# Seven 256-column products in place of eight in the output product of layer two, for the second to fourth block of tokens

## The chip, the cores and the metric

The kernel runs on one core of one Trainium2 chip. The time is that of one execution on the device, in microseconds (us); the median of three runs of the kernel before is 1085.78 us (1084.87 to 1085.96). The engines are named as the profile names them: PE is TensorE (matmul), PEld its weight loads, DVE VectorE, ACT ScalarE, POOL GpSimd, and SPq the queue of SyncE, from which nearly all transfers are started.

## The reference

Attention with a compressive memory gives 2304 tokens of 512 features; two gated layers follow. The change lies in the last line, the product of layer two's 1536 gated features with `w_out`.

```python
def _moe_ref(x, w_gate, w_val, w_out):          # layer one; 2304 tokens, 512 -> 1536 -> 512
    gate = 1.0 / (1.0 + np.exp(-(x @ w_gate)))
    val = x @ w_val
    return (gate * val @ w_out).astype(np.float32)

def _moe2_ref(x, w_a, w_b, w_out):              # layer two, same sizes
    a = x @ w_a
    b = x @ w_b
    return (a * b @ w_out).astype(np.float32)

def reference(**kwargs):
    ...
    x = _moe_ref(x=x, **moe_kwargs)
    return _moe2_ref(x=x, **moe2_kwargs)
```

## The kernel before

**Tiling.** The tokens are cut into five blocks: four of 512 (one per batch row) and a fifth of 256, which holds the first 64 tokens of each of the four. The 1536 inner features are twelve chunks of 128. Every fp32 operand is split into a high part (a rounded copy, written by ACT) and a low part (the rest, a subtraction on DVE), both in one "unit" of 128 x 2 x 512 values; each product is then three matmuls, high by high, high by low and low by high. PE's order is written out by hand (`manual_schedule`); on the other engines a scheduler sets the order of what the program records.

**Stages.** The attention fills the first 330 us. From there PE does the two layers. The input products of both layers are already done with seven products for eight (`strassen`, over pairs of token blocks, pairs of chunks and halves of the features); the gated features go out to DRAM tensors `gd` and come back for the output product. Weights come in pieces (`piece`: a transfer into `st`, two ACT operations, two DVE operations, an addition on POOL (L850), then the high part by ACT (L811) and the low part by DVE (L805)). Tasks like these are advanced from `hook`, which the PE program calls between its products; `ev`, `tile_t` and `bank` hand out the 10 buffers of gated features and results, the 11 work tiles and the 8 PSUM banks.

**The output product of layer two** is `outs(1, ...)`. It goes through the five blocks, and in each through the twelve chunks. `g_load` (L1230) brings a chunk of 128 features by 512 tokens back from `gd`, `g_split` cuts it into high part (ACT, L1237) and low part (DVE, L1238), up to three chunks ahead of the PE. `out_rows` (L1254 to L1256) then does, for each of the four groups of 128 tokens (two in the fifth block), three matmuls: the token group is the stationary operand, and all 512 output features of the weight chunk are the moving one.

```python
for f, o in enumerate(mo):
    r = slice(f * P, f * P + P)
    pe.matmul(o, lhsT=t[:, 0, r], rhs=w[:, 0], start=first, stop=False)
    pe.matmul(o, lhsT=t[:, 0, r], rhs=w[:, 1], start=False, stop=False)
    st["gate"] = pe.matmul(o, lhsT=t[:, 1, r], rhs=w[:, 0], start=False, stop=last)
```

The four PSUM banks of a block stay open over all twelve chunks; `c_fin` then copies them out (ACT L1321, DVE L1319) and sends them to the output (L1324). This stage runs from 927.7 us to the end of the span.

Of the kernel before, what the change touches and what calls it, by code (L numbers as in the profile page):

```python
# [9 lines left out]
F32 = mybir.dt.float32  # L10
# [9 lines left out]
def kernel(  # L20
# [721 lines left out]
    with tc.manual_schedule(engines={mybir.EngineType.PE}):  # L742
# [71 lines left out]
        def piece(layer, c, kind, half, mixed):  # L814
# [44 lines left out]
                return  # L859
            yield (half, 0, 0, 2)  # L860
            t = high_part(f"w{kind}", f, half)
            yield (0, 0, 0)
            low_part(t, f)
            ws[layer, c, kind] = t
            freed.append("t")

        uses, due, behind, held = {}, {}, [], []

        def used(key):
            uses[key] -= 1  # L870
# [12 lines left out]
        def mix(layer, g, kind):  # L883
            ka, kb = (layer, g, kind), (layer, g + MATE[layer], kind)
            yield (0, 2, 0)
            a, b, x, y = wf[ka], wf[kb], slice(0, 256), slice(256, 512)
            m, n = tile_t("mx"), tile_t("mx")
            vec.tensor_tensor(out=m[:, x], in0=b[:, x], in1=a[:, x], op=ALU.subtract)
            vec.tensor_tensor(out=n[:, x], in0=b[:, y], in1=b[:, x], op=ALU.subtract)
            yield (0, 0, 0)  # L890
            vec.tensor_tensor(out=n[:, y], in0=b[:, y], in1=m[:, x], op=ALU.subtract)
            vec.tensor_tensor(out=m[:, y], in0=a[:, y], in1=n[:, y], op=ALU.subtract)
            for key, f in (((layer, g, kind, 0), n), ((layer, g, kind, 1), m)):
                wf[key], uses[key], due[key] = f, 1, turn_[0] + 1
            used(ka)
            used(kb)

        def x_load(layer, b, kk):
            t = tile_t("xt")
# [332 lines left out]
        def g_split(layer, blk, c):  # L1232
# [5 lines left out]
            vec.tensor_tensor(  # L1238
                out=t[:, 1, 0:n], in0=f, in1=t[:, 0, 0:n].bitcast(F32), op=ALU.subtract
            )  # L1240

# [15 lines left out]

        def outs_of(layer):

            return [(blk, c) for blk in range(B + 1) for c in (every if layer else upper)]  # L1260

        def outs(layer, rate):

            seq = outs_of(layer)
            ahead = 2
            for m, (blk, c) in enumerate(seq):
                if m + 5 < len(seq):
                    g_load(layer, *seq[m + 5])
                while ahead < min(m + 4, len(seq)):
                    settle_free()  # L1270
                    key = (layer, seq[ahead][1], 2)
# [3 lines left out]
                    g_split(layer, *seq[ahead])  # L1275
                    ahead += 1
                if c == seq[0][1]:
                    mo = [bank() for f in range(KD if not layer else cols(blk) // P)]
                t, n = gs.pop((layer, blk, c)), cols(blk)
                if layer:  # L1280
                    out_rows(mo, c, t, c == 0, c == NCH - 1)
                else:
                    st["gate"] = out_wide(
                        blk, mo, c, t[:, 0, 0:n], t[:, 1, 0:n], c == MA, c == NCH - 1
                    )
                drop(t)
                if blk == B:
                    drop(ws[layer, c, 2])
                if c == NCH - 1:
                    (c_fin if layer else b_fin)(blk, mo)  # L1290
                hook(rate)

        def part_fin(blk, mo):
# [115 lines left out]
            wave(1, g)  # L1409
        for c in every:  # L1410
            task(piece(1, c, 2, "LH"[c % 2], False))

        ends = []
        early(B - 1, 4)
        early(B, 2)
        for layer in H2:
            for g, h in PAIRS[layer]:
# [10 lines left out]
            outs(layer, 6 if layer else 3)  # L1428
        bctx.close()


# [29 lines left out]
```

## Time and profile before

| | us |
|---|---|
| median of 3 runs | 1085.78 (1084.87 to 1085.96) |
| the profiled execution | 1085.2 |
| its span, first to last instruction | 1083.4 |
| PE busy | 1055.7 (97%) |
| DVE busy | 664.9 (61%) |
| ACT busy | 552.2 (51%) |
| POOL busy | 193.6 (18%) |
| layer two's output product, 927.7 us to the end | 155.7 |

The profile's busy time of a matmul includes the time in which its results drain while the next one already runs, so the pace of PE is read from the distance between starts and not from a single duration. The same holds for operations that stand back to back on DVE and ACT. An idle time in brackets behind a row of the timeline names what ended it.

### The profile page before, as it was taken

The numbers are of one execution on the slowest core, as the hardware profiler recorded it, in microseconds if no ns is written. First come the engines' busy times: TensorE is split into PE (matmuls) and PEld (weight loads), VectorE is DVE, ScalarE is ACT, GpSimd is POOL, SyncE is SP. The second block draws the span as 40 slices with busy tenths as digits, with TensorE's granted clock in tenths as the row PEclk, the third lists the DMA queues.
The fourth block names the chain that finished last, engine by engine and source line by source line (L and its number), as shares of the span: only waits on it lengthen the run. The fifth ranks groups of instructions, "written<-read, shape, count | busy, mean of one in ns | idle before, by whom it ended". The sixth has DMA issues, their size and how long they took to land.

```text
span 1083.4 us, 16215 instructions
## 1 busy us (share of the span) xinstructions
PE 1055.7 (97%) x5624; PEld 844.6 (78%) x5624; DVE 664.9 (61%) x1407; ACT 552.2 (51%) x1173; POOL 193.6 (18%) x204
## 2 busy tenths in 40 slices
PE   6989999999999999999999999999999999999997
PEld 4656677777777888888888888888888888888886
DVE  5897764565443988576578554976565578721221
ACT  5887765765744565544555333554344446431221
POOL 2443431232220302110221000221011013200000
PEclk9999999999999999999999999999999999999999
DMA  7665434333114434232368745343243244542233
GB/s 167 154 172 156 121 93 109 82 85 91 45 67 128 139 115 134 94 122 102 127 217 291 256 145 175 127 129 106 74 136 116 69 145 177 190 155 95 81 112 92
DMA packets 147202, 140.61 MB, mean 130 GB/s; under 512 B 73776, under 2 KB 107696, under 8 KB 147120
## 3 DMA queue, kind: packets, MB, share of 16 engines
q1 hardware_dynamic: 145648, 139.25, 41.0%
q8 instruction: 44, 0.72, 0.3%
q10 hardware_dynamic: 1472, 0.33, 0.1%
q14 instruction: 38, 0.31, 0.1%
HBM read 97.00 MB, written 42.54 MB: 129 GB/s over the span
## 4 chain that ended last, share of the span: by engine, by line
PE 82%; DVE 8%; ACT 3%; DMA 3%; issue 1%; POOL 1%; SPq 1%; POOLq 0%; DVEq 0%; ACTq 0%
PE gv L450 16%; PE gv L451 16%; PE gv L449 15%; PE gv L1256 5%; PE gv L1255 5%; PE gv L1254 4%; PE sc L195 4%; PE m L449 3%; PE tp L369 3%; PE m L451 3%; PE m L450 3%; PE tp L330 2%; PE tp L343 2%; DVE s L224 2%; PE tp L363 1%
## 5 line engine op out<-in xcount | busy, mean ns | idle before, releaser
L450 PE MATMUL gv<-xm,w 128*128 128x512 f32 (+1 forms) x752 | 272.7, 363 | 1.0 <-DVE xm L805 1.0
L451 PE MATMUL gv<-xm,w 128*128 128x512 f32 (+1 forms) x752 | 272.7, 363 | 0.0
L449 PE MATMUL gv<-xm,w 128*128 128x512 f32 (+1 forms) x752 | 272.3, 362 | 0.0
L850 POOL TENSOR_TENSOR wt<-wt,st 128x512 int32<-128x512 int32 x60 | 89.3, 1495 | 528.7 <-DVE wt L846 294.5
L450 PEld LDWEIGHTS gv<-xm,w 128*128 128x128 f32 x752 | 141.5, 188 | 24.1 <-DVE xm L805 1.5
L449 PEld LDWEIGHTS gv<-xm,w 128*128 128x128 f32 x752 | 141.5, 188 | 22.8 <-ACT ev L1069 0.4
L451 PEld LDWEIGHTS gv<-xm,w 128*128 128x128 f32 x752 | 141.6, 188 | 22.0
L1069 ACT ACTIVATE ev<-gv 128x512 f32<-128x512 f32 (+1 forms) x168 | 91.2, 561 | 85.2 <-PE gv L451 84.9
L1073 DVE TENSOR_TENSOR ev<-gv,ev 128x512 f32<-128x512 f32 x120 | 80.6, 685 | 70.3 <-PE gv L451 39.0
L1238 DVE TENSOR_TENSOR gs<-ev,gs 128x512 fp32r<-128x512 f32 (+1 forms) x100 | 63.4, 664 | 52.7 <-ACT gs L1237 52.2
L1237 ACT ACTIVATE gs<-ev 128x512 fp32r<-128x512 f32 (+1 forms) x100 | 56.1, 584 | 72.8 <-DMA ev<-gd 46.0
L1256 PE MATMUL gv<-w,gs 128*128 128x512 f32 x216 | 85.5, 396 | 0.1
L1255 PE MATMUL gv<-w,gs 128*128 128x512 f32 x216 | 85.0, 394 | 0.0
L1254 PE MATMUL gv<-w,gs 128*128 128x512 f32 x216 | 84.2, 390 | 0.0
L229 ACT ACTIVATE s<-s,mx 128x320 f32<-128x320 f32 (+3 forms) x128 | 77.6, 607 | 10.3 <-DVE mx L224 10.2
L224 DVE CUSTOM_DVE_ANT_0 s<-sc,mask 64x64 f32<-64x64 f32 (+4 forms) x160 | 68.9, 481 | 16.3 <-PE sc L195 16.3
L149 ACT ACTIVATE aw<-tp 128x512 f32<-128x512 f32 (+2 forms) x112 | 55.6, 513 | 43.7 <-PE tp L330 36.9
L840 ACT ACTIVATE wt<-st 128x512 f32<-128x512 f32 x60 | 39.5, 667 | 58.7 <-DMA st<-in_moe_w_out_dram 19.6
L195 PE MATMUL sc<-kt,qt 64*128 64x320 f32 (+4 forms) x384 | 61.4, 433 | 1.0 <-DVE mx L224 1.0
L451 PE MATMUL gv<-gs,w 128*128 128x512 f32 (+1 forms) x160 | 59.6, 373 | 0.0
L450 PE MATMUL gv<-gs,w 128*128 128x512 f32 (+1 forms) x160 | 59.4, 371 | 0.0
L449 PE MATMUL gv<-gs,w 128*128 128x512 f32 (+1 forms) x160 | 58.9, 368 | 0.0
(134 smaller groups left out, 1824.2 us busy)
## 6 DMA issues: line engine op xcount, KB each, us to landing
gd<-ev SPq DMA_DIRECT2D x80, 256.0 KB
ev<-gd SPq DMA_DIRECT2D x80, 256.0 KB
st<-in_moe_w_out_dram SPq DMA_DIRECT2D x24, 512.0 KB
st<-in_moe_w_gate_dram SPq DMA_DIRECT2D x12, 512.0 KB
st<-in_moe_w_val_dram SPq DMA_DIRECT2D x12, 512.0 KB
st<-in_moe_w_a_dram SPq DMA_DIRECT2D x12, 512.0 KB
st<-in_moe_w_b_dram SPq DMA_DIRECT2D x12, 512.0 KB
x<-rd SPq DMA_DIRECT2D x32, 144.0 KB
```

The source lines that it names most:

```text
L195: st["anchor"] = pe.matmul(scs[e][0:m, SC0[i] + a:SC0[i] + z], lhsT=st["q", p][r, r0:r0 + m], rhs=st["k", p][r, a:z], start=True, stop=True,)
L224: st["pace"] = vec.tensor_tensor_reduce(out=s, in0=scs[e][0:m, SC0[i]:SC0[i] + w], in1=mask[0:m, c:c + w], scale=1.0, scalar=BIG, op0=ALU. ...
L229: st["apace"] = act.activation(out=o, in_=s, func=AF.Exp, scale=-1.0, bias=mx[0:m, i:i + 1], accum_out=sms[p % 2][0:m, i:i + 1, e],)
L449: pe.matmul(o, lhsT=w[:, 0, ws_], rhs=xh, start=first, stop=False, skip_group_check=True)
L450: pe.matmul(o, lhsT=w[:, 0, ws_], rhs=xl, start=False, stop=False, skip_group_check=True)
L451: return pe.matmul(o, lhsT=w[:, 1, ws_], rhs=xh, start=False, stop=last, skip_group_check=True)
L850: pool.tensor_tensor(out=c32, in0=c32, in1=lo, op=ALU.add)
L1069: act.activation(out=t[:, 0:n], in_=src[:, 0:n], func=func)
L1073: st["gate"] = vec.tensor_tensor(out=t, in0=src, in1=t, op=ALU.add)
L1254: pe.matmul(o, lhsT=t[:, 0, r], rhs=w[:, 0], start=first, stop=False)
L1255: pe.matmul(o, lhsT=t[:, 0, r], rhs=w[:, 1], start=False, stop=False)
L1256: st["gate"] = pe.matmul(o, lhsT=t[:, 1, r], rhs=w[:, 0], start=False, stop=last)
```

## The change

Only layer two's output product is changed, and in it only the second, third and fourth block. A pair of chunks g and g + 6 is taken together: the two chunks, the two halves of the block's tokens (256 each) and the two halves of the output features (256 each) make a two by two by two block product, which takes eight half products in the form before and seven in the new one (Winograd's form). Each of the seven has its own PSUM bank, open over the six pairs of a block; in a bank, two groups of 128 tokens by 256 features lie side by side. A half product is two token groups by three matmuls of 256 columns, so a pair is 42 matmuls of 256 columns (`seven`, L1355) where it was 24 of 512. The first and the fifth block keep `out_rows`.

What goes with it:

- `mix_out`: for each of the six pairs, two mixed weight units (`wo`), from four 256-wide DVE operations (L911, L912, L915, L916), two high parts and two low parts. Their input, the weights in fp32, is kept in new DRAM tensors: `piece` stores it to `wd` (L863, behind the POOL addition), and `mix_out` loads it again (L907, L908). The six tasks may start from the second chunk of the first block on.
- `halves` in place of `g_split`: two mixed tiles u and v from four 256-wide DVE operations (L1324 to L1327), then high and low parts (L1331, L1332) of 256 columns for the first chunk and of 512 for the second chunk, u and v. The loads run two pairs ahead, `halves` one pair ahead.
- `seven_fin` in place of `c_fin`: in the last pair of a block each bank is taken out as soon as its product ends: one ACT copy (`keep`), seven DVE additions from PSUM (L1377), eight stores of 128 x 256 to the output (L1383).

```diff
+            if layer:
+                nc.sync.dma_start(out=wd[c], in_=f)
+                due[layer, c, kind] = turn_[0] + 3
...
+        def mix_out(g):
+            h = g + MATE[1]
+            yield (0, 4, 0)
+            a, b, m, n = (tile_t("mo") for _ in range(4))
+            x, y = slice(0, 256), slice(256, 512)
+            nc.sync.dma_start(out=a, in_=wd[g])
+            nc.sync.dma_start(out=b, in_=wd[h])
+            yield (0, 0, 0, 2)
+            with tc.issue_after(st["split"].ins):
+                vec.tensor_tensor(out=m[:, x], in0=a[:, y], in1=a[:, x], op=ALU.subtract)
+                vec.tensor_tensor(out=n[:, y], in0=b[:, y], in1=a[:, y], op=ALU.subtract)
+            yield (0, 0, 0)
+            with tc.issue_after(st["split"].ins):
+                vec.tensor_tensor(out=n[:, x], in0=b[:, y], in1=m[:, x], op=ALU.subtract)
+                vec.tensor_tensor(out=m[:, y], in0=b[:, x], in1=n[:, x], op=ALU.subtract)
+            freed.extend("tt")
+            for k, f in enumerate((n, m)):
...
+                t = high_part("wo", f, "H")
...
+                low_part(t, f)
+                wo[g, k] = t
...
+        def halves(blk, g):
...
+            vec.tensor_tensor(out=v[:, x], in0=a[:, y], in1=b[:, y], op=ALU.add)
+            vec.tensor_tensor(out=u[:, x], in0=v[:, x], in1=a[:, x], op=ALU.subtract)
+            vec.tensor_tensor(out=u[:, y], in0=a[:, x], in1=a[:, y], op=ALU.subtract)
+            vec.tensor_tensor(out=v[:, y], in0=b[:, x], in1=u[:, x], op=ALU.subtract)
+            gs[1, blk, g] = []
+            for f, n in ((a, 256), (b, 512), (u, 512), (v, 512)):
+                t = take("gs", "A")
+                act.activation(out=t[:, 0, 0:n], in_=f[:, 0:n], func=AF.Copy)
+                vec.tensor_tensor(
+                    out=t[:, 1, 0:n], in0=f[:, 0:n], in1=t[:, 0, 0:n].bitcast(F32),
+                    op=ALU.subtract,
+                )
...
+            jobs = (
+                (1, a, 0, wg, 0), (6, u, 0, n, 0), (2, b, 0, wh_, 0), (7, u, 256, n, 256),
+                (5, v, 0, m, 0), (3, v, 256, wh_, 256), (4, b, 256, m, 256),
+            )
+            for k, (i, t, at_, w, wc) in enumerate(jobs):
...
+                for r in H2:
+                    q_ = slice(at_ + r * P, at_ + r * P + P)
+                    for z, (th, wl_) in enumerate(((0, 0), (0, 1), (1, 0))):
+                        st["gate"] = pe.matmul(
+                            mo[i][:, 256 * r:256 * r + 256], lhsT=t[:, th, q_],
+                            rhs=w[:, wl_, wc:wc + 256], start=first and not r and not z,
+                            stop=last and r == 1 and z == 2, skip_group_check=True,
+                        )
+                if last:
+                    seven_fin(blk, i, mo)
...
+                while loaded < len(seq) and loaded <= m + (5 if len(seq[loaded]) == 2 else 2):
...
+                while ahead < loaded and ahead <= m + (3 if len(seq[ahead]) == 2 else 1):
```

**PE, where the first block ends and the second begins.** `gv` are PSUM banks, `w2` the weight chunks, `gs` the split features, `wo` the mixed weights. Before:

```order
L1255 MATMUL gv_9419<-w2_9372,gs_9553 128x512
L1256 MATMUL gv_9419<-w2_9372,gs_9553 128x512
L1254 MATMUL gv_9636<-w2_8884,gs_9570 128x512
L1255 MATMUL gv_9636<-w2_8884,gs_9570 128x512
L1256 MATMUL gv_9636<-w2_8884,gs_9570 128x512
```

and now (L1282 to L1284 are `out_rows`):

```order
L1283 MATMUL gv_9443<-w2_9395,gs_9617 128x512
L1284 MATMUL gv_9443<-w2_9395,gs_9617 128x512
L1355 MATMUL gv_9757<-w2_8896,gs_9687 128x256 x6
L1355 MATMUL gv_9764<-wo_9561,gs_9693 128x256 x6
L1355 MATMUL gv_9771<-w2_9263,gs_9690 128x256 x6
L1355 MATMUL gv_9778<-wo_9561,gs_9693 128x256 x6
L1355 MATMUL gv_9789<-wo_9605,gs_9696 128x256 x6
L1355 MATMUL gv_9796<-w2_9263,gs_9696 128x256 x6
L1355 MATMUL gv_9803<-wo_9605,gs_9690 128x256 x6
L1355 MATMUL gv_9757<-w2_9109,gs_9745 128x256 x6
L1355 MATMUL gv_9764<-wo_9563,gs_9751 128x256 x6
```

The second block's work is now seven rows of six narrow matmuls a pair, into seven banks; the second pair begins with the row before the last.

**DVE, at the same place.** The two COPY rows take the first block's results out of PSUM, so whatever stands behind them comes after that block's last matmuls. Before:

```order
L1238 TENSOR_TENSOR gs_9633<-ev_9585,gs_9633 128x512
L1319 COPY ev_9622<-gv_9417 128x512
L1319 COPY ev_9628<-gv_9419 128x512
L1238 TENSOR_TENSOR gs_9671<-ev_9631,gs_9671 128x512
L1238 TENSOR_TENSOR gs_9688<-ev_9652,gs_9688 128x512
```

and now (`gs_9751` and `gs_9754` are u and v of the second pair):

```order
L916 TENSOR_TENSOR mo_9731<-mo_9730,mo_9732 128x256
L1474 COPY ev_9714<-gv_9441 128x512
L1474 COPY ev_9720<-gv_9443 128x512
L805 TENSOR_TENSOR wo_9723<-mo_9567,wo_9723 128x512
L805 TENSOR_TENSOR wo_9810<-mo_9613,wo_9810 128x512
L1324 TENSOR_TENSOR ev_9740<-ev_9677,ev_9679 128x256
L1326 TENSOR_TENSOR ev_9739<-ev_9677 128x256
L1325 TENSOR_TENSOR ev_9739<-ev_9740,ev_9677 128x256
L1327 TENSOR_TENSOR ev_9740<-ev_9679,ev_9739 128x256
L805 TENSOR_TENSOR wo_9812<-mo_9655,wo_9812 128x512
L1332 TENSOR_TENSOR gs_9751<-ev_9739,gs_9751 128x512
```

Between the copies and the second pair's u stand three low parts of mixed weights and four mixing operations, where there was one low part per chunk before.

**The queue of SP, about the end of the input products.** `wd` is the new store of fp32 weights, `mo` its loads. Now:

```order
L863 DMA wd9_3925<-wt_9291 128x512
L1187 DMA gd1_1_5_3985<-ev_9352 128x512
L1258 DMA ev_9432<-gd1_0_5_3973 128x512
L1187 DMA gd1_3_5_4009<-ev_9381 128x512
L863 DMA wd10_3926<-wt_9314 128x512
L1258 DMA ev_9456<-gd1_0_6_3974 128x512
L863 DMA wd11_3927<-wt_9317 128x512
L1243 DMA gd1_4_11_4027<-ev_9413 128x256
L1258 DMA ev_9485<-gd1_0_7_3975 128x512
```

The `wd` rows are new in this queue; the loads of the first block's sixth chunk onward (`gd1_0_5` and later) now stand behind stores that wait for POOL.

## Rows read from the trace of the kernel before

**Rows 1.** The page: busy time by engine; the chain that ended last.

```profile
PE 1055.7 (97%) x5624; PEld 844.6 (78%) x5624; DVE 664.9 (61%) x1407; ACT 552.2 (51%) x1173; POOL 193.6 (18%) x204
PE 82%; DVE 8%; ACT 3%; DMA 3%; issue 1%; POOL 1%; SPq 1%; POOLq 0%; DVEq 0%; ACTq 0%
```

**Rows 2.** Busy time by stretch, columns in the first line; layer two's output product.

```profile
core 0: us, PE busy (x) PEld busy (x) DVE busy (x) ACT busy (x) POOL busy (x), PEclk, DMA share, GB/s
927.70:950.00 22.30, 22.20 (x98) 17.82 (x97) 14.50 (x22) 10.27 (x19) 3.04 (x2) 1.00 0.50 167
950.00:960.90 10.90, 10.90 (x49) 8.87 (x48) 0.63 (x1) 0.60 (x1) 0.00 (x0) 1.00 0.00 0
961.50:994.70 33.20, 33.20 (x146) 26.98 (x145) 9.29 (x14) 8.60 (x15) 0.00 (x0) 1.00 0.36 126
```

**Rows 3.** The chain in order of time (start, us, what), twelve chunks apart.

```profile
964.61 0.24 PE gv L1255
...
997.85 0.24 PE gv L1255
```

**Rows 4.** Layer one's fifth block (256 columns): busy time, PE's timeline; a page group.

```profile
651.24:662.73 11.49, 11.49 (x97) 11.47 (x96) 2.96 (x8) 1.25 (x3) 0.00 (x0) 1.00 0.31 101
651.25 0.28 PE L449 MATMUL gv<-gs,w 128*128 128x256 f32 x1
...
662.73 0.40 PE L449 MATMUL gv<-xm,w 128*128 128x512 f32 x1
...
L450 PEld LDWEIGHTS gv<-xm,w 128*128 128x128 f32 x752 | 141.5, 188 | 24.1 <-DVE xm L805 1.5
```

**Rows 5.** Waits of PE after 880 us; DVE's row that ended it.

```profile
PEld gv L1256 <- DVE gs L1238: 0.5, 1, 0.5
929.49 1.80 DVE L1238 TENSOR_TENSOR gs<-ev,gs 128x512 fp32r<-128x512 f32 x1
```

**Rows 6.** DVE's timeline (start, us, operation, count): single operations and runs of them.

```profile
811.60 0.41 DVE L892 TENSOR_TENSOR mx<-wt,mx 128x256 f32<-128x256 f32 x1
811.94 0.41 DVE L891 TENSOR_TENSOR mx<-wt,mx 128x256 f32<-128x256 f32 x1
812.38 0.43 DVE L892 TENSOR_TENSOR mx<-wt,mx 128x256 f32<-128x256 f32 x1
...
823.74 0.69 DVE L1073 TENSOR_TENSOR ev<-gv,ev 128x512 f32<-128x512 f32 x1 [0.68 <-PE gv L451]
824.47 0.69 DVE L1077 TENSOR_TENSOR ev<-ev 128x512 f32<-128x512 f32 x1
...
932.14 1.28 DVE L1238 TENSOR_TENSOR gs<-ev,gs 128x512 fp32r<-128x512 f32 x2
933.35 0.68 DVE L805 TENSOR_TENSOR w<-wt,w 128x512 fp32r<-128x512 f32 x1
933.95 3.69 DVE L1238 TENSOR_TENSOR gs<-ev,gs 128x512 fp32r<-128x512 f32 x6
```

**Rows 7.** DVE's timeline at the end of the first block.

```profile
943.60 1.29 DVE L1238 TENSOR_TENSOR gs<-ev,gs 128x512 fp32r<-128x512 f32 x2 [2.28 <-ACT gs L1237]
960.27 0.69 DVE L1319 COPY ev<-gv 128x512 f32<-128x512 f32 x1 [15.38 <-PE gv L1256]
961.64 0.69 DVE L1319 COPY ev<-gv 128x512 f32<-128x512 f32 x1 [0.68 <-PE gv L1256]
```

**Rows 8.** ACT's timeline, high parts in the first block.

```profile
930.77 0.63 ACT L811 ACTIVATE w<-wt 128x512 fp32r<-128x512 f32 x1
931.31 2.18 ACT L1237 ACTIVATE gs<-ev 128x512 fp32r<-128x512 f32 x4
934.94 1.20 ACT L1237 ACTIVATE gs<-ev 128x512 fp32r<-128x512 f32 x2 [1.46 <-DMA ev<-gd]
```

**Rows 9.** POOL's last additions, and the queue of SP behind them.

```profile
924.38 2.32 POOL L850 TENSOR_TENSOR wt<-wt,st 128x512 int32<-128x512 int32 x1 [10.48 <-DMA gd<-ev]
927.33 3.41 POOL L850 TENSOR_TENSOR wt<-wt,st 128x512 int32<-128x512 int32 x2 [0.63 <-DVE wt L846]
926.52 0.42 SPq L1230 DMA_DIRECT2D ev<-gd  x1
928.84 0.91 SPq L1230 DMA_DIRECT2D ev<-gd  x2
932.02 4.40 SPq L1230 DMA_DIRECT2D ev<-gd  x9
```

**Rows 10.** The end: the last matmul, and what follows it.

```profile
1077.58 0.40 PE L1256 MATMUL gv<-w,gs 128*128 128x512 f32 x1
1077.94 2.44 SPq L1328 DMA_DIRECT2D out_dram<-ev  x4
1078.01 0.69 DVE L1319 COPY ev<-gv 128x512 f32<-128x512 f32 x1 [8.73 <-PE gv L1256]
```

More of the change, by code (lines that the diff above doesn't have):

```diff
@@ L865, in piece @@
             freed.append("t")
-        uses, due, behind, held = {}, {}, [], []
+        uses, due, behind, held, wo = {}, {}, [], [], {}
+        wd = [dram.tile([P, 512], F32, name=f"wd{c}") for c in every]
         def used(key):
@@ L1237, in g_split @@
             act.activation(out=t[:, 0, 0:n], in_=f, func=AF.Copy)
-            vec.tensor_tensor(
+            st["split"] = vec.tensor_tensor(
                 out=t[:, 1, 0:n], in0=f, in1=t[:, 0, 0:n].bitcast(F32), op=ALU.subtract
@@ L1258, in outs_of, with outs @@
         def outs_of(layer):
-            return [(blk, c) for blk in range(B + 1) for c in (every if layer else upper)]
-        def outs(layer, rate):
-            seq = outs_of(layer)
+            return [(blk, c) for blk in range(1 if layer else B + 1) for c in (every if layer else upper)]
+        def outs(rate):
+            seq = outs_of(0)
             ahead = 2
@@ L1274, in outs @@
                     need(lambda: key in ws and units_left(half_of(ws[key])))
-                    g_split(layer, *seq[ahead])
+                    g_split(0, *seq[ahead])
                     ahead += 1
                 if c == seq[0][1]:
[L1278 to L1285, printed above, removed]
+                    mo = [bank() for f in range(KD)]
@@ new lines, in outs2 @@
+        def outs2(rate):
+            seq = [(0, c) for c in every]
+            seq += [(blk, g, "pair") for blk in range(1, B) for g, h in PAIRS[1]]
+            seq += [(B, c) for c in every]
+            loaded, ahead = 5, 2
+            for m, x in enumerate(seq):
+                blk, c = x[:2]
+                if m == 1:
+                    late["outs"] = True
+                while loaded < len(seq) and loaded <= m + (5 if len(seq[loaded]) == 2 else 2):
+                    y = seq[loaded]
+                    g_load(1, *y[:2])
+                    if len(y) > 2:
+                        g_load(1, y[0], y[1] + MATE[1])
+                    loaded += 1
+                while ahead < loaded and ahead <= m + (3 if len(seq[ahead]) == 2 else 1):
+                    settle_free()
+                    y = seq[ahead]
+                    key = (1, y[1], 2)
+                    if len(y) > 2:
+                        need(lambda: all((y[1], k) in wo for k in H2) and units_left("A") > 3)
+                        halves(*y[:2])
+                    else:
+                        if ahead > m + 2 and not (key in ws and units_left(half_of(ws[key]))):
+                            break
+                        need(lambda: key in ws and units_left(half_of(ws[key])))
+                        g_split(1, *y)
+                    ahead += 1
+                if len(x) > 2:
+                    if c == 0:
+                        mo = {}
+                    seven(blk, c, mo, rate)
+                    continue
+                if c == 0:
+                    mo = [bank() for f in range(cols(blk) // P)]
+                t = gs.pop((1, blk, c))
+                out_rows(mo, c, t, c == 0, c == NCH - 1)
+                drop(t)
+                if blk == B:
+                    drop(ws[1, c, 2])
+                if c == NCH - 1:
+                    c_fin(blk, mo)
@@ L1411 @@
             task(piece(1, c, 2, "LH"[c % 2], False))
+        for g, h in PAIRS[1]:
+            task(mix_out(g), lambda g=g: "outs" in late and all(
+                due.get((1, c, 2), 1 << 30) <= turn_[0] for c in (g, g + MATE[1])
+            ))
         ends = []
@@ L1427 @@
                 group(layer, g, 1, rate)
-            outs(layer, 6 if layer else 3)
+            outs2(6) if layer else outs(3)
         bctx.close()
```

64 lines of the change are left out of this document (60 added, 4 removed).

## Prediction

> **What bounds the kernel now.** I read the page's busy times and its chain first: PE is busy 97% of the span and holds 82% of the chain [rows 1]. Then the busy times by stretch for the stage that changes: in all of layer two's output product PE is busy without a gap, the clock is granted in full, and the other engines have room; a block of 33.2 us needs 9.3 us of DVE and 8.6 us of ACT [rows 2]. So the second to fourth block cost what PE takes for their matmuls. Its pace is read from starts: twelve chunks further on in the chain, the same matmul starts 997.85 - 964.61 = 33.24 us later [rows 3]. Twelve chunks are 144 matmuls of 512 columns, so one takes 0.2308 us. The only wait of PE in the stage is 0.5 us in the first block, on a DVE subtraction that took 1.80 us [rows 5].
>
> **Narrow matmuls.** The term on which all rests is the pace at 256 columns with a weight load before each. The trace has it: layer one's fifth block runs 96 such matmuls from 651.25 to 662.73 [rows 4], 11.48 / 96 = 0.1196 us each. The operands have the same form as in the new code (fp32r, 128 x 128 stationary, 256 moving, half a bank written), and a new tile is waited for there too without a visible gap. A pair of chunks goes from 24 x 0.2308 = 5.54 us to 42 x 0.1196 = 5.02 us, a block from 33.24 to 252 x 0.1196 = 30.14 us. That is 3.10 us a block and **9.3 us for three**. It is less than an eighth of 99.7 us (12.5 us), since half the columns take 0.52 of the time; the other 3.2 us go there.
>
> The bounds of this term: at exactly half of 0.2308 (0.1154) it would be 12.5 us; if the excess over half, 0.0042 us, doubled in the new order, 252 x 0.1238 = 31.2 us a block and 6.1 us in all. I take the measured pace, as its row is the same operation.
>
> **What the cover must hide.** Everything else is added beside PE, on engines with room. Four places decide.
>
> *DVE in a full block.* Back to back, a 512-wide operation takes (3.69 - 0.69) / 5 = 0.60 us and a 256-wide one 811.94 - 811.60 = 0.34; where it reads what the one before it wrote, 812.38 - 811.94 = 0.44, or 824.47 - 823.74 = 0.73 at 512 [rows 6]. A pair needs five of 256 and three of 512: 5 x 0.34 + 2 x 0.10 for the dependent ones + 3 x 0.60 = 3.7 us of PE's 5.02. A block needs 6 x 3.7 = 22.2 plus seven additions from PSUM, at most 7 x 0.73 = 5.1: 27.3 us of 30.14. DVE thus goes from 28% to some 90%, still under PE. ACT has four copies a pair at (2.18 - 0.62) / 3 = 0.52 us [rows 8], about 2 us of 5.02.
>
> *DVE in the first block.* The mixing falls here. From 932.1 us, where DVE now does the first block's splits [rows 6], the new order has 51 rows up to the COPY rows: 21 of 512 (ten splits, six low parts of mixed weights, one of a plain one, four of the first two pairs) and 30 of 256: 12.6 + 10.2 + about 0.8 for dependent ones = 23.6 us. It ends at 955.7; the first COPY begins at 960.27 [rows 7], so 4.5 us are left, out of an idle time of 15.38 us before.
>
> *The second pair's u.* This is the tightest place, because the order puts it behind the COPY rows. The last COPY starts at 961.64 and gives DVE free at 962.24; two low parts (1.20), four mixing operations (1.36, with 0.2 for dependence), one low part (0.60) and u's own (0.60) end at 966.2. PE leaves the first block at about 961.45, needs 5.02 us for the first pair and 0.72 for the second pair's first product, which reads only a chunk that has long been split: u is wanted at 967.2. One us of slack; v, third and later pairs have 1.5 us and more.
>
> *Queues and banks.* The last `wd` stores wait for POOL, whose additions end at 926.7 and, two in 3.41 us from 927.33, at about 929.0 and 930.7 [rows 9]. Loads that stood at 926.52 and 928.84 move to about 927.5, 929.5 and 931; the chunks they bring are wanted by PE from 942 on, 2.77 us apart, so 10 us cover it. The twelve stores and twelve loads add 6 MB; the DMA share is 0.50 there and 0.36 after [rows 2]. Before the end of the input products the order of DVE and ACT differs only in a handful of neighbouring rows. Of the eight banks, seven are open; the next block's first product takes the eighth, its second the one that ACT copied four products earlier, and each later one follows an addition by 4 us. In the last pair DVE has 7 additions at 0.6 to 0.73 against products of 0.72 us, and keeps up. The fifth block and the 5 us of copy and store behind the last matmul [rows 10] are unchanged.
>
> So I cost all this at nothing but 0.5 us for places where it does not quite fit; if the cover at the second block's start were gone, it would cost as the first rival says.
>
> **The sum.** Against the profiled execution: 1085.2 - 9.3 + 0.5 = 1076.4. The median before lies 0.6 above that execution, so the forecast is 1077.0 us.
>
> **Rivals.**
>
> *DVE late at the second block.* DVE counts on 0.60 and 0.34. If the 51 rows take their full single durations instead (0.69 and about 0.42, rows as above), 21 x 0.09 + 30 x 0.08 = 4.3 us of the 4.5 are gone, and the same rows behind the COPY cost 0.6 of the 1 us. Waits between DVE and ACT come on top: a high part of mixed weights needs DVE's result, and its low part needs ACT's. In the trace DVE lost 2.28 us at one such place to a late load [rows 7], and ACT 1.46 [rows 8]; two or three of these would make PE wait 1.5 to 7 us in the second block. That gives 1078 to 1084. For it speaks how closely the new order is packed, against it the slack worked out above. Chance 0.22, about two thirds of it within the faster side.
>
> *DVE becomes the bound in all three blocks, and the kernel slower.* The mechanism is the hand-over inside a pair: mixing on DVE, high part on ACT, low part on DVE, in order on both. If nothing else fills DVE while ACT makes u and v high, a pair costs 5 x 0.42 + 3 x 0.69 = 4.17 us in full durations, two exposed ACT copies of 0.63 [rows 8], and 0.8 as a sixth of the additions: 6.2 us. A block would take 37.4 us, 4.1 more than now, and the kernel 1085.8 + 3 x 4.1 = 1098. It decides from 5.54 us a pair, so from 0.29 us exposed in each of the two hand-overs. Against it: the new order puts rows of the next pair between u's mixing and its low part nearly everywhere. Chance 0.06.
>
> *Weight loads that don't overlap.* In the 256-column stretch PEld shows as busy as PE, 11.47 of 11.49 us with 96 loads [rows 4], each 0.188 us long by the page's group but started every 0.1196, so they overlap one another or the matmuls; if in the new stage each took its 0.188 alone, a pair would cost 42 x 0.188 = 7.9 us, 2.36 more than now, 18 x 2.36 = 42 us in all: 1128. The rows speak against it, since loads of the same size kept the pace there. Chance 0.02.
>
> The Trainium skill has a rule that speaks against the change here: "TensorE: Matmul & The Clock Gate", Part 3, says that a weight load overlaps matmuls in flight only when it targets another row group, which full 128-row operands never do. By it (an estimate, with that page's load of 128 columns in 107 ns) 42 loads and half-width matmuls a pair would lose more than the columns save: 18 more loads, 1.9 us, against 0.7 us of columns, some 22 us over the 18 pairs. The trace does not bear it out: 0.1196 us is shorter than load and matmul one after the other could be. By that rule, the result would be slower than before.
>
> **How the numbers follow.** The forecast case (PE at 0.1196, at most 2 us of waits) has 0.70 and gives 1076 to 1079. The first rival adds 0.14 as faster and 0.08 within 0.2%, the other two 0.08 as slower. A change of 0.2% (2.2 us) is about what a measurement of this kernel can tell from none. Faster 0.84, same 0.08, slower 0.08. The range takes the forecast case and the nearer half of the first rival: 1075.5 (no wait at all, and the term a little over 9.3) to 1081.
>
> **What would show it.** Right: the new matmul row starts every 0.120 us and a block takes 30.1 to 30.5 us with PE busy throughout; DVE is some 25 to 27 us busy in it; PE's waits in the stage stay under 1 us. Wrong by the first rival: PE waits on DVE (a low part of u, v or mixed weights) just after the first block. By the second: such waits in every pair of all three blocks. By the third: narrow matmuls start 0.188 us or more apart with nothing waited for. If the first block's start is later than 927.7, the stores in the queue of SP have cost more than I allow.

## The result, and the profile after

The changed kernel takes 1076.41 us (median, 1074.53 to 1079.6) where the kernel before took 1085.87 in the same session: ratio 0.9912, 95% interval 0.9892 to 0.9931. The forecast was 1077.0. A second session gave 1075.86 us and a ratio of 0.9927 (0.991 to 0.9944). The profiled execution of the changed kernel took 1075.23 us, its span 1073.4.

The page's busy times, engine by engine (busy us, share of the span, instructions), to be held against [rows 1]:

```profile
PE 1045.6 (97%) x5948; PEld 852.9 (79%) x5948; DVE 729.0 (68%) x1566; ACT 572.0 (53%) x1218; POOL 193.9 (18%) x204
```

PE has 324 matmuls more and is 10.1 us less busy; DVE has 159 operations more and is 64.1 us busier. Busy time by stretch, with the columns of [rows 2], for the first block and the three changed ones:

```profile
926.50:961.20 34.70, 32.90 (x143) 26.47 (x142) 29.49 (x59) 15.66 (x29) 3.61 (x3) 1.00 0.57 195
961.45:991.60 30.15, 30.15 (x255) 30.14 (x254) 28.43 (x60) 16.20 (x32) 0.00 (x0) 1.00 0.45 143
991.60:1021.70 30.10, 30.10 (x256) 30.10 (x256) 26.19 (x57) 13.28 (x25) 0.00 (x0) 1.00 0.44 143
1021.70:1051.80 30.10, 30.10 (x253) 30.01 (x253) 23.16 (x51) 12.11 (x24) 0.00 (x0) 1.00 0.40 128
```

PE is busy throughout all three at the full granted clock, while DVE's share falls from 28.43 of 30.15 us in the first of them to 23.16 in the last: the first holds six low parts of mixed weights (4.1 us), the last the mixing for five pairs in place of six. PE's timeline (start, us, operation, count) at the two ends of the changed part:

```profile
961.23 0.39 PE L1284 MATMUL gv<-w,gs 128*128 128x512 f32 x1
961.46 0.89 PE L1355 MATMUL gv<-w,gs 128*128 128x256 f32 x6
962.19 0.87 PE L1355 MATMUL gv<-wo,gs 128*128 128x256 f32 x6
962.89 0.88 PE L1355 MATMUL gv<-w,gs 128*128 128x256 f32 x6
...
1050.60 0.88 PE L1355 MATMUL gv<-wo,gs 128*128 128x256 f32 x6
1051.32 0.40 PE L1282 MATMUL gv<-w,gs 128*128 128x512 f32 x1
```

From 961.46 to 1051.32 are 89.86 us for 756 matmuls, 0.1189 us each. Three blocks took 3 x 33.24 = 99.72 before, so they gain **9.86 us**; the forecast had 9.3.

The only wait of PE behind 880 us (waited for: us, times, longest), and DVE's row that ended it, against [rows 5]:

```profile
PE gv L1284 <- DVE gs L1266: 1.8, 1, 1.8
929.53 1.77 DVE L1266 TENSOR_TENSOR gs<-ev,gs 128x512 fp32r<-128x512 f32 x1
```

The 0.5 us in [rows 5] are those of the weight load (PEld), which waits 2.2 us now; PE's own idle time at this place was 0.1 us before. This execution began the stage at 926.17, 1.7 us earlier than the profiled one of before (927.86), but PE left the wait at 931.35, as it did then (931.34): at that place DVE sets the time, and its subtraction is slow (1.77 us for a 512-wide one) as it was in [rows 5]. So the first block is 35.29 us long instead of 33.59. The whole account of the stage, first to last matmul start: 149.72 us before, 141.64 now; 9.86 gained in three blocks, 1.70 lost in the first, 0.1 in the fifth. The 1.7 us earlier start can't be put down to the change: over the profiled executions of all kernels of this case the stage began anywhere between 922.98 and 929.95 us. For the same reason the start, which the prediction named as a sign of what the stores cost, says nothing here. Lengths within the stage are therefore compared below beside the times.

### The profile page after: what moved, and what is told of

Its sections match the earlier page's. It is cut to its first block, busy times and chain, and to the rows that moved or that the text cites. A ratio compares the mean times of both kernels' runs of the same rounds, so it can differ in the third digit from the quotient of the medians.

```text
span 1073.4 us, 17162 instructions
## 1 busy us (share of the span) xinstructions
PE 1045.6 (97%) x5948; PEld 852.9 (79%) x5948; DVE 729.0 (68%) x1566; ACT 572.0 (53%) x1218; POOL 193.9 (18%) x204
## 4 chain that ended last, share of the span: by engine, by line
PE 81%; DVE 8%; DMA 4%; ACT 3%; issue 2%; SPq 2%; POOL 1%; DVEq 0%; POOLq 0%; ACTq 0%
PE gv L450 15%; PE gv L451 15%; PE gv L449 15%; PE gv L1355 8%; PE sc L195 4%; PE m L449 3%; PE tp L369 3%; PE m L451 3%; PE m L450 3%; PE tp L330 2%; PE tp L343 2%; PE gv L1284 1%; PE gv L1283 1%; PE gv L1282 1%; PE tp L363 1%
## 5 line engine op out<-in xcount | busy, mean ns | idle before, releaser
L149 ACT ACTIVATE aw<-tp 128x512 f32<-128x512 f32 (+2 forms) x112 | 55.7, 514 | 43.6 <-PE tp L330 36.8
L1265 ACT ACTIVATE gs<-ev 128x512 fp32r<-128x512 f32 (+1 forms) x64 | 34.5, 558 | 60.6 <-DMA ev<-gd 31.2
L1266 DVE TENSOR_TENSOR gs<-ev,gs 128x512 fp32r<-128x512 f32 (+1 forms) x64 | 40.1, 648 | 35.3 <-ACT gs L1265 34.9
L1355 PE MATMUL gv<-wo,gs 128*128 128x256 f32 x432 | 60.1, 281 | 0.0
L841 ACT ACTIVATE st<-st 128x512 int32<-128x512 uint32 x60 | 40.0, 667 | 36.7 <-DMA st<-in_moe_w_a_dram 9.4
L1331 ACT ACTIVATE gs<-ev 128x512 fp32r<-128x512 f32 (+1 forms) x72 | 38.1, 571 | 38.8 <-DVE ev L1325 13.1
```

The costliest lines, as they stand in the source:

```text
L149: act.activation(out=out, in_=src, func=AF.Copy)
L1266: st["split"] = vec.tensor_tensor(out=t[:, 1, 0:n], in0=f, in1=t[:, 0, 0:n].bitcast(F32), op=ALU.subtract)
L1355: st["gate"] = pe.matmul(mo[i][:, 256 * r:256 * r + 256], lhsT=t[:, th, q_], rhs=w[:, wl_, wc:wc + 256], start=first and not r and not z, ...
```

## Experiments

Each edit is to the changed kernel unless said otherwise. "Block" is the distance between the first matmul starts of two blocks.

### The changed kernel again

> The changed kernel once more, beside the others on the same chip. Both theories: 1076 to 1077 us, some 9.5 us under the kernel before. Its trace shows again whether PE's only wait in layer two's output product is at the second chunk of the first block (1.8 us in the first trace).

1075.86 us (1073.52 to 1078.6). Three blocks took 90.38 us, the stage from first to last matmul 141.80. The stage began at 929.38 here. PE waited 1.44 us at the first block's second chunk and 0.19 at 972.76, on DVE's low part of the second pair's v (the matmul that waits is the 27th of that pair, the third of its fifth product, and the third matmul of a token group is the first to read a low part). The second of these waits doesn't occur in the other execution, and it stands where the forecast claimed "1.5 us and more" of slack.

### Seven products in the second block alone

```diff
-            if blk == B - 1:
+            if blk == 1:
...
-            seq += [(blk, g, "pair") for blk in range(1, B) for g, h in PAIRS[1]]
-            seq += [(B, c) for c in every]
+            seq += [(1, g, "pair") for g, h in PAIRS[1]]
+            seq += [(blk, c) for blk in range(2, B + 1) for c in every]
```

> Only the second block uses the seven products; the third and fourth go back to eight. Mixing of weights, its stores and loads stay. Theory (the gain is PE's columns, block by block, and all that is added is hidden): a third of the gain, 9.86 / 3 = 3.3 us, so 1082.3 to 1083 us, PE needing about 30.0 us for the second block and 33.2 for the others. Rival (a fixed part of the gain or loss sits elsewhere, such as in the earlier start of the stage seen in the first trace, or in mixing that is not quite hidden): clearly off a third, above 1084 if there is a fixed cost, below 1081 if there is a fixed gain.

1086.1 us (1081.55 to 1087.54), ratio 1.0012 (0.9999 to 1.0025): a third of the change brought nothing, where a third of its gain was expected. The second block took 33.71 us (961.28 to 994.99). PE's waits in it and the longer of the two in PE's timeline, DVE's timeline, the queue of SP, and busy time with the columns as above:

```profile
PE gv L1355 <- DVE gs L1332: 2.8, 2, 1.8
968.44 1.10 PE L1355 MATMUL gv<-wo,gs 128*128 128x256 f32 x8
971.36 0.74 PE L1355 MATMUL gv<-wo,gs 128*128 128x256 f32 x4 [1.82 <-DVE gs L1332]
```

```profile
965.99 0.68 DVE L805 TENSOR_TENSOR wo<-mo,wo 128x512 fp32r<-128x512 f32 x1
969.94 0.42 DVE L1324 TENSOR_TENSOR ev<-ev 128x256 f32<-128x256 f32 x1 [3.27 <-DMA ev<-gd]
970.62 1.29 DVE L1332 TENSOR_TENSOR gs<-ev,gs 128x512 fp32r<-128x512 f32 x2
```

```profile
960.04 1.13 SPq L1479 DMA_DIRECT2D out_dram<-ev  x2
961.22 0.44 SPq L1258 DMA_DIRECT2D ev<-gd  x1
961.75 0.88 SPq L1479 DMA_DIRECT2D out_dram<-ev  x2
962.68 12.50 SPq L1258 DMA_DIRECT2D ev<-gd  x7
```

```profile
961.00:970.00 9.00, 8.54 (x70) 8.26 (x69) 4.42 (x10) 3.07 (x7) 0.00 (x0) 1.00 0.87 283
```

The two loads of the third pair (the one at 961.22 and the first at 962.68) stand behind two and four of the first block's stores (L1479), with further loads at their heels, and the DMA share is 0.87 over these 9 us. The later one lands about 7 us after its issue; DVE is idle for 3.27 us before the third pair's mixing, and PE waits for what stands behind that on DVE: 1.82 us for the low part of the second pair's v (the eight matmuls before the wait are the fourth product's six and the fifth's first two) and 0.95 for that of the third pair's u. That is the first rival's outcome by another cause, a late transfer. The changed kernel has the same order, and a milder case (DVE's timeline, then busy time):

```profile
965.80 0.68 DVE L1332 TENSOR_TENSOR gs<-ev,gs 128x512 fp32r<-128x512 f32 x1
967.73 0.43 DVE L1324 TENSOR_TENSOR ev<-ev 128x256 f32<-128x256 f32 x1 [1.24 <-DMA ev<-gd]
...
968.40 1.02 DVE L1332 TENSOR_TENSOR gs<-ev,gs 128x512 fp32r<-128x512 f32 x2
...
971.29 0.68 DVE L1332 TENSOR_TENSOR gs<-ev,gs 128x512 fp32r<-128x512 f32 x1
```

```profile
961.20:970.20 9.00, 9.00 (x76) 8.93 (x75) 7.23 (x15) 4.66 (x9) 0.00 (x0) 1.00 0.87 288
```

The second pair's v, the first of the two at 968.40, is ready at 969.09 there, and u of the third pair at 971.97. PE's products that read them begin at 969.33 and 972.20, the matmuls that read the low parts 0.24 us later, so each has about half a microsecond to spare. Both kernels issue the later of the two loads 1.40 us after the block's start and have a DMA share of 0.87 over the 9 us; why DVE could go on 6.27 us after the block's start in this one and 8.66 in the other, the runs don't show.

### The same, with the third pair's loads one pair earlier

Added to the edit above:

```diff
-                while loaded < len(seq) and loaded <= m + (5 if len(seq[loaded]) == 2 else 2):
+                while loaded < len(seq) and loaded <= m + (5 if len(seq[loaded]) == 2 else 2 + (m == NCH - 1)):
```

> Only the second block takes the seven products, as in the run before that gained nothing (1086.1), and the third pair's loads are put into the queue one pair earlier. There the second block took 33.71 us, with the loads of its third pair landing 7 us after their issue and PE waiting 2.77 us on DVE. Theory: with the loads in time the block takes 30.0 to 30.6 us and the time is 1082.4 to 1083.4, 3 us under the kernel before. Rival (the burst of loads for the plain blocks that follow and the stores is late whatever the order): the block takes 32 us or more and the time stays at 1084.5 to 1086.5.

1083.24 us (1080.58 to 1085.52), ratio 0.9978 (0.9964 to 0.9993). PE has no wait behind 960, and its second block goes from 964.22 to 994.32, 30.10 us:

```profile
965.03 0.42 DVE L1324 TENSOR_TENSOR ev<-ev 128x256 f32<-128x256 f32 x1
...
966.97 0.42 DVE L1324 TENSOR_TENSOR ev<-ev 128x256 f32<-128x256 f32 x1
```

```profile
962.99 2.49 SPq L1479 DMA_DIRECT2D out_dram<-ev  x4
965.57 9.67 SPq L1258 DMA_DIRECT2D ev<-gd  x9
```

```profile
964.20:994.40 30.20, 30.20 (x254) 30.17 (x253) 27.17 (x56) 16.30 (x31) 0.00 (x0) 1.00 0.44 135
```

The four stores now stand together, the two loads ahead of them (18 of the stage's 60 loads, not 16, are issued by 958 us), and the third pair's mixing at 966.97 waits for nothing. The theory held in the block: it brings 33.24 - 30.10 = 3.1 us where its cover holds, and this was lost before to two loads that came late (the edit changes their place in the queue, and with it the order in which DVE mixes, but no work). The time lies in the theory's range and is 2.9 us under the run above, but only 1.4 us under the kernel before (1084.65 in that session), where 3 were expected. In the profiled execution the first block took the gain again: it is 37.07 us long (33.59 before), since PE waited 2.05 us at its second chunk, and behind that the granted clock was 0.50 from 935 to 937 us, where 512-column matmuls started 0.43 us apart:

```profile
934.05 0.63 PE L1283 MATMUL gv<-w,gs 128*128 128x512 f32 x1
934.47 0.63 PE L1284 MATMUL gv<-w,gs 128*128 128x512 f32 x1
```

### The changed kernel with the third pair's loads one pair earlier

> The loads of the second block's third pair are put into the queue of SP one pair earlier, ahead of the first block's stores to the output. In the changed kernel DVE waited 1.24 us for them at 967.73 and u of that pair was ready some 0.2 us before PE wanted it; in the two executions of the kernel that changed only one block, or were repeated, PE waited there 0.19 to 2.77 us. Theory (the loads stand late in the queue, and that is the tight place): DVE's wait for a DMA at that place goes from 1.24 us to under 0.3 us, PE has no wait between 960 and 985, and the time is the changed kernel's, 1075.9, less 0 to 0.5 us, since that kernel waited there little. Rival (the order of DVE's rows at the block's start is what is tight): with the third pair's mixing now recorded among the second pair's rows, the second pair's u comes later, PE waits 0.5 to 2 us on DVE between 964 and 970, and the time is 1076.5 to 1078.

1076.72 us (1070.58 to 1079.47), ratio 0.9915 (0.9891 to 0.9939). DVE's wait for a transfer is gone at this place, PE waits nowhere but at the second chunk (2.2 us), and three blocks take 89.87 us. u of the second pair came at 970.36 (969.67 + 0.69), with PE wanting it at 965.64 + 5.74 = 971.4, so the rival's wait did not come. The time lies in the rival's range and not in the theory's, but with runs from 1070.58 to 1079.47 it can't be told from the changed kernel's, which waited 0 and 0.19 us there.

### One operation more on DVE in each pair

The low part of b is written twice:

```diff
+                for again in range(2 if f is b else 1):
                     vec.tensor_tensor(
                         out=t[:, 1, 0:n], in0=f[:, 0:n], in1=t[:, 0, 0:n].bitcast(F32),
```

> Each pair has one more DVE operation of 512 columns (the low part of the second chunk is written twice, the same values): 6 x 0.60 = 3.6 us of DVE a block. Theory (DVE was busy 28.4, 26.2 and 23.2 of 30.1 us in the three blocks, so it is close behind PE but not the bound): the second block reaches 32.0 us of DVE and PE waits there for about 2 us, the other two stay at 30.1: 1077 to 1079.5 us. Rival one (DVE is already the bound): 3.6 us in each block, 1087 us. Rival two (DVE is far from the bound, its busy time is overlap): no change, 1076.4 us.

1081.8 us (1079.85 to 1085.75), ratio 0.9983 (0.9965 to 1.0), between the theory and the first rival. Three blocks take 96.86 us, 7.0 more than without it. PE waits 5.1 us in seven places, and DVE, though in want of time, idles as long for late loads (as it does in the changed kernel, where 5.1 us in three places cost PE nothing):

```profile
PE gv L1356 <- DVE gs L1333: 4.6, 6, 1.1
PE gv L1356 <- ACT gs L1331: 0.5, 1, 0.5
```

```profile
DVE ev L1324 <- DMA ev<-gd: 5.2, 3, 2.8
```

With the third pair's loads of the second block one pair earlier:

> One 512-wide operation more on DVE in each pair, as in the run that gave 1081.8, and the third pair's loads one pair earlier. There PE waited 2.54 us between 970 and 982, behind a wait of DVE of 2.82 us for the late loads. Theory (of the 5 us that operation cost, about half is that load, since DVE with no spare time can't make up for it): these waits go to 0.5 us or less, the three blocks take 94 to 95 us in place of 96.9, and the time is 1079 to 1080.5. Rival (DVE is simply full): its work is the same, the three blocks take 96.5 to 97.5 us, and the time stays at 1081 to 1082.5.

1080.76 us (1079.21 to 1082.99), ratio 0.9964 (0.9947 to 0.9982). The theory held in the trace: the waits between 960 and 1005 are gone, and three blocks take 93.92 us, 2.9 less. The time is 0.3 us above the theory's range, and its difference from the run above, 1 us, is less than the spread of either. What is left are 1.69 us in the third block, behind 2.43 us in which DVE waited for a load that was not moved, and 1.5 in the fourth, behind a high part of ACT that had waited 1.64 us for PE. The second block is the telling row:

```profile
962.80:993.00 30.20, 30.20 (x256) 30.20 (x255) 29.92 (x63) 16.81 (x32) 0.00 (x0) 1.00 0.36 118
```

DVE is busy for 29.92 of 30.20 us and PE does not wait once. So DVE's work may come up to PE's pace there; what DVE can no longer make good is a late transfer.

### Three operations more on DVE in each pair

Four writes of the same low part in place of one.

> Three more DVE operations of 512 columns a pair (the low part of the second chunk written four times over): 10.8 us of DVE a block, 39, 37 and 34 us in all. Theory (DVE becomes the bound once it has more than PE's 30.1 us): the three blocks take 34 to 39 us each, 9 + 7 + 4 = 20 us more, 1094 to 1098 us, PE waiting for a DVE low part in nearly every pair. Rival (waits elsewhere, hand-overs with ACT or loads, set the pace of DVE, and additions fill its gaps): under 1088 us.

1097.71 us, beside 1083.06 for the kernel before on the same chip (one execution of each, as in the two other experiments that have this 1083.06). Three blocks take 116.4 us, 26.5 more than in the changed kernel where the theory had 20, with PE waiting 17.3 us on DVE in six places, not in nearly every pair, and the mean granted clock 0.91 to 0.96 in them. This is the second rival's outcome: a kernel that is slower than before, reached with 18 x 3 operations more.

### The mixing of weights five chunks later

```diff
-                if m == 1:
+                if m == 6:
                     late["outs"] = True
```

> The mixing of weights may start at the seventh chunk of the first block instead of the second, 5 x 2.77 = 13.8 us later. Theory (the mixing is hidden only because it starts early; DVE had 4.9 us of idle time left in the first block): DVE is still mixing when the second block is due, and PE waits 5 to 10 us there, on low parts of mixed weights or of the second pair: 1081 to 1086 us. Rival (only the first two pairs' mixed weights are wanted at once, the rest can follow during the second block): PE waits under 2 us and the time is 1076 to 1078.5 us.

1081.38 us, beside the same 1083.06. PE waits 2.3 us on DVE in the changed blocks (at 976.88 and 1007.95), and three blocks take 93.07 us, 2.7 to 3.2 more than with the mixing in time. So the place of the mixing matters, but less than the theory had it: the waits are nearer to the rival's "under 2 us" than to 5 to 10. That the time still reaches the theory's range is owed to the first block, 36.8 us long: after the second chunk's wait of 1.76 us the granted clock fell. By stretch:

```profile
933.80:936.70 2.90, 2.90 (x8) 2.31 (x7) 2.90 (x6) 0.63 (x1) 0.00 (x0) 0.50 0.98 299
937.00:960.00 23.00, 23.00 (x101) 18.73 (x101) 18.72 (x44) 8.66 (x15) 0.00 (x0) 1.00 0.51 173
```

### The first two chunks of the stage loaded and split one product earlier

```diff
-                    if last and x is both[1] and i in (3, 4):
-                        for key in outs_of(layer)[:2] if i == 3 else outs_of(layer)[2:4]:
+                    if last and x is both[1] and i in (7, 3, 4):
+                        for key in outs_of(layer)[:2] if i == 7 else outs_of(layer)[2:4] if i == 4 else ():
...
-                        if i == 4:
+                        if i == 3:
```

> The loads and the split of the first two chunks of the output product are recorded one and two products earlier in the last pair of input products, so that on ACT the high part of the second chunk stands ahead of a weight piece that waits for POOL. Theory (that wait of 1.8 us is a place in a queue, and DVE has room behind it): the wait at the second chunk is under 0.3 us and the time 1 to 1.8 us under the changed kernel, 1074.6 to 1075.6 us. Rival (DVE as a whole is late there, so the wait only moves to the third or fourth chunk): 1076 to 1077 us and a wait of 1.5 us or more at a later chunk.

1075.66 us (1073.9 to 1078.69), ratio 0.9924 (0.9907 to 0.9942). The wait at the second chunk is gone. One of 0.26 us stands at the third chunk (before the stage's 27th matmul), so the wait moved on, as the rival had it, but nearly all of it went on the way. Another of 0.28 stands at the second pair's v, and the stage is 140.71 us long in place of 141.64 and 141.80. The microsecond is there in the trace; in the time it can't be told from none.

Both small repairs together:

> The changed kernel with both small repairs: the first two chunks of the stage split two turns earlier, and the third pair's loads ahead of the stores. Theory: PE waits under 0.5 us in the whole stage, first to last matmul of the stage 140.4 to 140.8 us (141.6 and 141.8 in the two executions of the changed kernel), and the time is 1074.5 to 1075.5. Rival (what the stage saves there is lost again in the variation of the stages before): the time is 1075.5 to 1076.5, not to be told from the changed kernel's.

1074.98 us (1074.03 to 1079.84), ratio 0.9913 (0.9892 to 0.9934). PE waits once, 0.96 us, again at the third chunk and not the second, and the stage is 140.85 us long. The length comes within 0.1 us of the theory, the wait does not; the time is inside the theory's, yet an interval of over 4 us leaves it undecided. Less its waits, the stage is 139.8 to 140.2 us in all five executions with three changed blocks and no added work (141.64 - 1.80, 141.80 - 1.63, 142.05 - 2.21, 140.71 - 0.54, 140.85 - 0.96), so there is no more than that wait left to win here.

### 128 columns

All pairs but the first of each block move 128 columns in place of 256, so half of each of these products is left out and the sums are incomplete.

```diff
+            wide = 256 if first else 128
...
-                            mo[i][:, 256 * r:256 * r + 256], lhsT=t[:, th, q_],
-                            rhs=w[:, wl_, wc:wc + 256], start=first and not r and not z,
+                            mo[i][:, 256 * r:256 * r + wide], lhsT=t[:, th, q_],
+                            rhs=w[:, wl_, wc:wc + wide], start=first and not r and not z,
```

> In all pairs but a block's first, the seven products move 128 columns instead of 256 (half of those output columns are left without five sixths of their sum); matmuls and weight loads stay 42 a pair. Theory (the 256-column matmul is set by its columns): six matmuls take 0.36 to 0.45 us where they took 0.71, and DVE, at 23 to 28 us a block, becomes the bound: a block 24 to 29 us, 1065 to 1073 us in all. Rival (a weight load before each matmul sets the pace at 256 columns): six matmuls still take 0.70 us or so, and the time stays at 1076 us.

1112.86 us, beside 1083.06 for the kernel before: less work, and slower. PE's timeline in three places:

```profile
973.54 0.66 PE L1356 MATMUL gv<-wo,gs 128*128 128x128 f32 x4 [2.05 <-DVE gs L1332]
974.04 0.83 PE L1356 MATMUL gv<-w,gs 128*128 128x128 f32 x6
...
976.90 1.48 PE L1356 MATMUL gv<-wo,gs 128*128 128x128 f32 x6
978.18 1.48 PE L1356 MATMUL gv<-w,gs 128*128 128x128 f32 x6
...
1014.13 1.48 PE L1356 MATMUL gv<-w,gs 128*128 128x256 f32 x6
1015.41 1.89 PE L1356 MATMUL gv<-wo,gs 128*128 128x256 f32 x12
1017.14 0.88 PE L1356 MATMUL gv<-w,gs 128*128 128x256 f32 x6
...
1021.86 0.83 PE L1356 MATMUL gv<-w,gs 128*128 128x128 f32 x6
1022.53 0.84 PE L1356 MATMUL gv<-wo,gs 128*128 128x128 f32 x6
```

and by stretch:

```profile
976.00:1012.00 36.00, 36.00 (x171) 36.00 (x170) 22.09 (x46) 10.91 (x22) 0.00 (x0) 0.50 0.21 67
1020.00:1042.00 22.00, 22.00 (x200) 22.00 (x198) 16.76 (x36) 8.22 (x17) 0.00 (x0) 1.00 0.22 61
```

At the full clock groups of six matmuls of 128 columns start 0.67 us apart (0.1117 for one) where six of 256 need 0.71 to 0.72: half the columns save 6%. The theory's pace fell, the rival's held nearly (its time did not): from 256 to 128 columns the time of a matmul hardly falls. That the weight load sets it, as the rival had it, was not shown. The loss of time is the clock's: the trace shows 0.50 (1.2 GHz) for the 36 us from 976 to 1012 and again from 1056 to 1086, behind waits of 2.05 and 0.53 us.

## Why the prediction was right

**The pace.** The term on which all rested held: the same operation elsewhere in the trace, 0.1196 us [rows 4], against 0.1189 here. That is 9.86 us in place of 9.3 (9.34 in the second execution), well inside the bounds of 6.1 and 12.5. The excess over half of 0.2308 is 0.0035 us, a little less than the 0.0042 taken. That the gain lies in the blocks' matmuls is shown by the single block: 3.1 us where its cover held.

**The third rival**, weight loads that don't overlap, is out: 42 loads of 0.19 us and 42 matmuls pass in 5.0 us. So is, for this kernel, the rule of the Trainium skill ("TensorE: Matmul & The Clock Gate", Part 3) that was set beside it: by the estimate there the kernel would have been some 22 us slower. What the runs show in its place is a pace of 0.112 us at 128 columns, with 256 just above it; what sets that pace they don't show.

**DVE in a full block.** 27.3 us forecast as a sum; 28.43, 26.19 and 23.16 us measured, the first of them with the last low parts of mixed weights, which the sum left out. "25 to 27" was too low for that one and too high for the last. A busy share of 94% cost nothing, as taken.

**DVE in the first block.** It ended the mixing at 958.95, not at 955.7:

```profile
951.29 0.69 DVE L1266 TENSOR_TENSOR gs<-ev,gs 128x512 fp32r<-128x512 f32 x1 [3.34 <-ACT gs L1265]
...
958.52 0.43 DVE L916 TENSOR_TENSOR mo<-mo 128x256 f32<-128x256 f32 x1
960.28 0.69 DVE L1474 COPY ev<-gv 128x512 f32<-128x512 f32 x1 [1.34 <-PE gv L1284]
```

The sum of the work was right and 3.34 us of idle time came on top, behind a split that ACT began late; what ACT waited for the profile doesn't name. Of the 4.5 us of slack 1.3 were left. The late mixing, which takes that slack away, cost 2.3 us of waits: the slack was needed.

**The tightest place.** The second pair's u was forecast for 966.2 and came at 966.48, for a want at 967.2. That step held. But the tightest places are the second pair's v and the third pair's u, for which the text had "1.5 us and more" without a working: half a microsecond each in the profiled execution, and less than none for v in the second one. Both stand on DVE behind the third pair's first mixing, which waited for its loads. The step that failed is the one on queues: it costed the `wd` stores ahead of the stage, which came where they were forecast (926.75, 929.08 and 930.77), and not that the loads of the third pair stand behind the first block's stores. In the changed kernel this cost 0 to 0.2 us; with plain blocks behind it 2.8 us of waits and the whole gain. That it cost so little here is in part luck. The first rival was nearer than its working says: that has slow operations and hand-overs between DVE and ACT, and a late load only as an example from another place (2.28 us).

**The second chunk's wait** was forecast to stay (all waits under 1 us) and was 1.8 and 1.44 us: that sign of being right failed. In the profiled execution PE waits 1.7 us longer than before, as much as the stage began earlier, since DVE's subtraction ended at the same time as before. But in the second one the stage began later than before (929.38), and PE waited all the same. In the ten profiled executions that keep this order it was 0.9 to 2.2 us, in the one of the kernel before 0.1. So the first block costs 1.3 to 1.7 us, where 0.5 was set aside for all places together. Why DVE is late against PE there no run shows; splitting earlier leaves 0.26 and 0.96 us of it, at the third chunk.

**The sum.** From its first to its last matmul start the stage is 8.1 and 7.9 us shorter in the two executions, where the sum had 8.8. In the first of them the changed blocks brought 0.6 more than forecast and the first block cost 1.2 more than the 0.5. That the profiled execution still came to 1075.2, where 1076.4 was summed, is owed to the stage's earlier start (1.7) and a shorter end (0.2). The medians, 9.5 and 8.6 us under those of the kernel before, hold such differences too, so the mechanism is right and the pace well forecast, while the closeness of 1077.0 to the median is in part luck.

## What to carry to other kernels

Take the pace of a narrower matmul from a stretch that runs the same operation, as starts divided by count; half the columns are not half the time, and going on from 256 to 128 columns saved only 6% here. Where an engine is filled to 90% and more by work that depends on loads, its slack hangs on when these loads land: count what is issued ahead of each of them at the switch between stages, move the load if a store stands there, and look at what stands behind the waiting operation on the same engine, since that is late too. A gain that a part of a change fails to show may be lost at the seam and not absent; look for the wait at the seam before the mechanism is given up.

## What the runs showed beside that

**A wait costs PE more than its idle time.** Three blocks with one more operation a pair are 7.0 us longer, of which 5.15 are listed as waits in seven places; the remaining 1.9 us are 0.27 a wait. One such place, in the run with one operation more (PE's timeline):

```profile
968.83 0.52 PE L1356 MATMUL gv<-wo,gs 128*128 128x256 f32 x3
970.35 0.74 PE L1356 MATMUL gv<-wo,gs 128*128 128x256 f32 x4 [1.00 <-DVE gs L1333]
970.93 0.88 PE L1356 MATMUL gv<-w,gs 128*128 128x256 f32 x6
```

Without the wait the fourth matmul would start at 968.83 + 3 x 0.119 = 969.19; it starts 1.16 us later, and the next three lose another 0.1.

**The granted clock after a wait.** Behind waits of 1.80 and 1.44 us in the changed kernel, and of 2.21 with the third pair's loads earlier, the clock stayed at 1.00 (2.4 GHz). With the mixing later it fell to 0.50 (1.2 GHz) after one of 1.76 us at the same place, seven 512-column matmuls started 0.43 us apart, and by 937.1 it was back; in the single block with earlier loads it did the same after 2.05 us. With 128 columns it fell after 2.05 and after 0.53 us and stayed at 0.50 while PE was busy without a gap, for at least 36 and 30 us; the first time it came back between 1015.4 and 1017.1, after the next block's 256-column matmuls had begun. From 1020 to 1042, with matmuls of 128 columns and no wait, it was 1.00. At 0.50 six matmuls take 1.28 us at 128 columns (976.90 to 978.18) and at 256 alike (1014.13 to 1015.41), so there half the columns save nothing. What decides whether it falls was not settled.
